# First token chunk of an attention + gated-MLP kernel: transposes in PSUM tiles of their own, the third block's statistics later, the first norm in one piece

## Chip, core and metric

The kernel runs on one core of one Trainium2 chip. The metric is the device time of one launch in microseconds (us), as the median of several runs. The kernel before was run six times: median 316.49, lowest 315.66, highest 317.83 us. The execution that was profiled is the one of 315.66 us; from its first to its last instruction, its span, it took 313.9 us, so 1.8 us of a run lie outside the span.

The engines are called by the profile's names: PE is TensorE (matmuls and transposes), PEld its weight loads, DVE is VectorE, ACT is ScalarE, POOL is GpSimd, and SP is the engine that issues most DMAs.

## What is computed

Input is `x` (2048 tokens of 640 features, bf16), normalised over the features, and then used in two branches, whose sum is added to `x`:

```python
xn = _layernorm(x)                              # (x - mean) / sqrt(var + 1e-5)
qkv = xn @ wqkv                                 # 32 heads of 20, q, k, v
scores = q @ k.T * 20 ** -0.5                   # each token sees itself and the 255 before it
o = softmax(masked scores) @ v
attention = o @ wo
g, u = xn @ w_gate, xn @ w_up                   # 640 -> 1536
mlp = (sigmoid(g) * u) @ w_down
out = x + attention + mlp
```

## The kernel before, in words

The 2048 tokens go through in four chunks of 512 (`CW`), each chunk in four blocks of 128 tokens (`SBC`). For the matmuls the normalised tokens must lie with features on the partitions: `xnT[c]`, 128 features x 5 groups x 512 tokens. For chunks 1 to 3 DMA transposes make it, beside other work. For chunk 0 nothing else is there to do yet, and the head of the program makes it on PE: this head is what the change is about.

The order of every engine's instructions is the order in which the Python code calls them (`tc.manual_schedule()`, L147), and each engine runs its own strictly in order. Tile pools only place buffers and add the waits: an instruction waits for the others that still use the tile that it writes or reads.

The head (L604 to L644) treats the four blocks of chunk 0 as follows.

- Mean and variance. Blocks 0 and 2 have theirs from DVE: two `bn_stats` of 320 features each (`ln_half`, L249) and one `bn_aggr` (`ln_mv`, L254); then ACT takes the square root (`root`, L579), and DVE the reciprocal (`norm`, L583). Blocks 1 and 3 have theirs from ACT: `mean_act` (L589, a copy that also sums), `root_act` (L594 and L595, squares and a root); DVE's reciprocal is at L599.
- The normalisation itself is one DVE `tensor_scalar` (L269 for blocks 0 and 2, L600 for 1 and 3) into `xn`. For block 0 it is cut in two pieces, features 0 to 383 and 384 to 639.
- `transpose_rows` (L275) has PE transpose the 128 x 128 squares of a block into PSUM, and `copy_rows` (L278) copies the result to `xnT`, with DVE or, for block 1, with ACT. For block 0 this goes in two rounds: three squares and their copy, then two squares and theirs.
- `project_v` (L324): for each block two groups of five matmuls that give the V columns 0 to 319 and 320 to 639 (`hf` 0 and 1), and `copy_v` (L331), which brings them to SBUF with DVE or ACT.

All transposes of the head write one PSUM tile, `home` (L608): 128 x 4 x 1024 bf16, 8 KB in each partition, so 2 KB for each block. It uses the buffer that the attention scores have later (pool `ps_s`, L145; tag "ps").

The inputs come by DMA (L173 to L201): block 0 of `x` on SP, blocks 1 and 2 on ACT, then on SP the V columns 0 to 319 of `wqkv`, block 3, the V columns 320 to 639, the q columns, the k columns, the first halves of `w_gate` and `w_up`, and two clears of scratch in DRAM.

After the head, PE makes q and k of chunk 0 without a pause: `g_qk(0)`, L298, 50 matmuls. Their results go through five SBUF buffers (`st`) to DRAM scratch (`sq`, `sk`, L306) and back in another layout (`qT`, `kT`, L313). Then gate and up matmuls (L398, L405) follow, and from L465 on the attention scores, mixed with matmuls of the other parts by a list with costs (`Fill`, L526). The change doesn't touch that part.

The lines of the head in their order, which is also DVE's, ACT's and PE's order:

```python
mv0 = ln_block(0, 0)                                  # L609
...
half2 = ln_half(0, 2, 0)                              # L612
r1 = root_act(1, xn1, neg1)
norm(0, mv0, r0, ((0, 3 * P), (3 * P, D)))            # L614
for lo, hi in ((0, 3), (3, DC)):
    transpose_rows(0, home, lo, hi)
    copy_rows(0, home, dve, lo, hi)
...
mv2 = ln_mv(ln_half(0, 2, 1, half2))                  # L623
```

Of the kernel before, what the change touches and what calls it, by code (L numbers as in the profile page):

```python
# [9 lines left out]
P = 128  # L10
S = 2048
D = 640
# [3 lines left out]
DC = D // P  # L16
FC = F // P
CW = 512
NCH = S // CW
SBC = CW // P  # L20
HG = 4
# [9 lines left out]
MULT = mybir.AluOpType.mult  # L31
SUB = mybir.AluOpType.subtract
POW = mybir.AluOpType.pow
GE = mybir.AluOpType.is_ge
BF16 = mybir.dt.bfloat16
FP32 = mybir.dt.float32
# [71 lines left out]
def kernel(  # L108
# [11 lines left out]
    nc = tc.nc  # L120
# [21 lines left out]
    ps_a = pool("ps_a", 1, space=bass.MemoryType.PSUM)  # L142
    ps_d = pool("ps_d", 3, space=bass.MemoryType.PSUM)
    banks = ctx.enter_context(ExitStack())
    ps_s = banks.enter_context(tc.tile_pool(name="ps_s", bufs=1, space=bass.MemoryType.PSUM))  # L145

    ctx.enter_context(tc.manual_schedule())  # L147

# [1 line left out]
    xc = {}  # L150

    def load_x(c):
        t = xp.tile([P, SBC, D], BF16, name="xc")
        xc[c] = t
        nc.sync.dma_start(out=t, in_=xr[:, c * SBC:(c + 1) * SBC, :])
# [73 lines left out]
    ident = const.tile([P, P], BF16, name="ident")  # L229
# [7 lines left out]
    for n in (6, 5):  # L237
        ps = ps_d.tile([P, CW], FP32, name="pwarm", tag="d")
# [4 lines left out]
    xnT = {}  # L243
    xns = {}

    def ln_half(c, s, a, stats=None):
        if a == 0:
            stats = lnp.tile([P, 2, nc.vector.BN_STATS_DIM], FP32, name="stats")
        nc.vector.bn_stats(out=stats[:, a, :], in_=xc[c][:, s, a * HALF:(a + 1) * HALF])  # L249
        return stats  # L250

    def ln_mv(stats):
        mv = lnp.tile([P, nc.vector.BN_AGGR_DIM], FP32, name="mv")
        nc.vector.bn_aggr(out=mv, in_=stats)  # L254
        return mv

    def ln_block(c, s):
        return ln_mv(ln_half(c, s, 1, ln_half(c, s, 0)))
# [4 lines left out]
        nc.gpsimd.tensor_tensor(out=rstd, in0=rstd, in1=neghalf, op=POW)  # L263
        return rstd

    def norm_block(c, s, mv, rstd, cuts=((0, D),)):
        xn = lnp.tile([P, D], BF16, name="xn", bufs=5)
        for a, b in cuts:
            nc.vector.tensor_scalar(out=xn[:, a:b], in0=xc[c][:, s, a:b], scalar1=mv[:, 0:1],  # L269
                                    scalar2=rstd[:, 0:1], op0=SUB, op1=MULT)  # L270
        xns[c, s] = xn

    def transpose_rows(s, home, lo=0, hi=DC):
        for d in range(lo, hi):
            nc.tensor.transpose(home[:, s, d * P:(d + 1) * P], xns[0, s][:, d * P:(d + 1) * P], ident)  # L275

    def copy_rows(s, home, copy, lo=0, hi=DC):
        copy(out=xnT[0][:, lo:hi, s * P:(s + 1) * P],  # L278
             in_=home[:, s, lo * P:hi * P].rearrange("p (d t) -> p d t", t=P))

    def turn_block(c, s):
        nc.sync.dma_start(out=xnT[c][:, :, s * P:(s + 1) * P], in_=xns.pop((c, s)), transpose=True)
# [8 lines left out]
    def proj_block(w, c, m):  # L291


        base = 0 if w == "q" else D
        ps = ps_d.tile([P, CW], FP32, name="pqk", tag="d")
        for d in range(DC):
            wt = wqkv[:, d, base:base + D].rearrange("p (k m) -> p m k", m=DC)
            nc.tensor.matmul(ps, lhsT=wt[:, m, :], rhs=xnT[c][:, d, :],  # L298
                             start=(d == 0), stop=(d == DC - 1))
        st = stp.tile([P, CW], BF16, name="st")  # L300
        if w == "q":
            nc.vector.tensor_copy(out=st, in_=ps)
        else:
            nc.scalar.copy(out=st, in_=ps)
        dst = scratch[w, c % 2].rearrange("(h j) s -> h j s", j=32)
        nc.sync.dma_start(out=dst[:, 4 * m:4 * m + 4, :], in_=st)  # L306

    def spread(w, c, g0, g1):

        if g0 == 0:  # L310
            qk[w, c] = (qp if w == "q" else kp).tile([P, NG, CW], BF16, name=w + "T")
        src = scratch[w, c % 2].rearrange("(g p) s -> p g s", p=P)
        nc.sync.dma_start(out=qk[w, c][:, g0:g1, :], in_=src[:, g0:g1, :])  # L313
# [7 lines left out]
    def project_v(c, s, hf):  # L321
        ps = ps_d.tile([P, CW], FP32, name="pv", tag="d")
        for d in range(DC):
            nc.tensor.matmul(ps[:, 0:HALF], lhsT=xnT[c][:, d, s * P:(s + 1) * P],  # L324
                             rhs=wqkv[:, d, 2 * D + hf * HALF:2 * D + (hf + 1) * HALF],
                             start=(d == 0), stop=(d == DC - 1))
        return ps
# [34 lines left out]
    def g_qk(c):  # L362
        for w in "qk":
            for m in range(DC):
                proj_block(w, c, m)
                if c == 0 and w == "q" and m == 1:
                    load_x(1)
                if w == "k" and m == 1:
                    spread("q", c, 0, NG if c else 2)
                yield 5 * MM  # L370
        if c == 0:
            spread("k", c, 0, 1)
            spread("k", c, 1, 3)
            spread("q", c, 2, 4)
            spread("k", c, 3, 4)
# [81 lines left out]

    def scores(c, step):
        pt = pp.tile([P, HG, PTW], BF16, name="pT")
        ps = ps_s.tile([P, HG, CW], FP32, name="ps", tag="ps")  # L460
        for g, hf, r, q, n, col in step["scores"]:
            kc, kb = divmod(c * SBC + r, SBC)
            key = kb * P + hf * U
            for i in range(HG):
                nc.tensor.matmul(  # L465
                    ps[hf * U:(hf + 1) * U, i, col * U:(col + n) * U],
                    lhsT=qk["k", kc][32 * i:32 * i + DH, g, key:key + U],
                    rhs=qk["q", c][32 * i:32 * i + DH, g, q * U:(q + n) * U],
                    start=True, stop=True)
        nc.scalar.activation(out=pt[:, :, 0:CW], in_=ps, func=EXP, scale=SCALE)  # L470

        def keep(out, in_, n, width, base, sign):
            nc.gpsimd.affine_select(out=out, in_=in_, pattern=[[0, HG], [0, n], [sign, width]],  # L473
                                    compare_op=GE, fill=0.0, base=base, channel_multiplier=-sign)

        def spans(u, n, units):
            a, b = divmod(u, SPAN)
            two = pt.rearrange("p h (a b) -> p h a b", a=2)
            return two[:, :, a:a + n, b * U:(b + units) * U]

        if "late" in step:
            src, to, n = step["late"]
            keep(pt[:, :, to * U:(to + n) * U].rearrange("p h (n u) -> p h n u", u=U),
                 spans(src, n, 1), n, U, -1 - U, -1)
            u, n = step["oldest"]
            keep(spans(u, n, 1), spans(u, n, 1), n, U, -1, -1)
            keep(spans(step["diag"], 2, 2), spans(step["diag"], 2, 2), 2, P, 0, 1)
        return pt
# [88 lines left out]
    def root(mv):  # L577
        r = lnp.tile([P, 1], FP32, name="rstd")
        nc.scalar.activation(out=r, in_=mv[:, 1:2], func=SQRT, bias=eps)  # L579
        return r  # L580

    def norm(s, mv, r, cuts=((0, D),)):
        nc.vector.reciprocal(r, r)  # L583
        norm_block(0, s, mv, r, cuts)

    def mean_act(s):
        xn = lnp.tile([P, D], BF16, name="xn", bufs=5)
        neg = lnp.tile([P, 1], FP32, name="neg")
        nc.scalar.activation(out=xn, in_=xc[0][:, s, :], func=IDENTITY, scale=-1.0 / D, accum_out=neg)  # L589
        return xn, neg  # L590

    def root_act(s, xn, neg):
        r = lnp.tile([P, 1], FP32, name="rstd")
        nc.scalar.activation(out=xn, in_=xc[0][:, s, :], func=SQUARE, bias=neg, accum_out=r)  # L594
        nc.scalar.activation(out=r, in_=r, func=SQRT, bias=eps, scale=1.0 / D)  # L595
        return r
# [8 lines left out]
    for s in range(SBC):  # L605
        new_v(0, s)
    act, dve = nc.scalar.copy, nc.vector.tensor_copy
    home = ps_s.tile([P, HG, 2 * CW], BF16, name="pt", tag="ps")  # L608
    mv0 = ln_block(0, 0)  # L609
    xn1, neg1 = mean_act(1)  # L610
    r0 = root(mv0)
    half2 = ln_half(0, 2, 0)  # L612
    r1 = root_act(1, xn1, neg1)
    norm(0, mv0, r0, ((0, 3 * P), (3 * P, D)))  # L614
    for lo, hi in ((0, 3), (3, DC)):
        transpose_rows(0, home, lo, hi)
        copy_rows(0, home, dve, lo, hi)
    v00 = project_v(0, 0, 0)
    norm_act(1, xn1, neg1, r1)
    xn3, neg3 = mean_act(3)  # L620
    transpose_rows(1, home)
    copy_rows(1, home, act)
    mv2 = ln_mv(ln_half(0, 2, 1, half2))  # L623
    r2 = root(mv2)
    v01 = project_v(0, 0, 1)
    copy_v(0, 0, 0, v00, dve)
# [1 line left out]
    r3 = root_act(3, xn3, neg3)  # L628
    v10 = project_v(0, 1, 0)
    copy_v(0, 0, 1, v01, dve)  # L630
    transpose_rows(2, home)
    copy_rows(2, home, dve)
    v11 = project_v(0, 1, 1)
    norm_act(3, xn3, neg3, r3)
    copy_v(0, 1, 0, v10, act)
    copy_v(0, 1, 1, v11, act)
    v20 = project_v(0, 2, 0)
    transpose_rows(3, home)
    copy_rows(3, home, dve)
    copy_v(0, 2, 0, v20, act)  # L640
    proj_v(0, 2, 1, dve)
    proj_v(0, 3, 0, act)
    proj_v(0, 3, 1, dve)
    nc.scalar.activation(out=scr, in_=neghalf, func=EXP)  # L644
    for _ in g_qk(0):
        pass
    load_rest()
# [37 lines left out]
    cuts = [(ends[n, NG - 1] + 2, f"out{n}") for n in range(NCH - 1)] + [(len(todo), None)]  # L685
# [23 lines left out]
    c = NCH - 1  # L709
# [17 lines left out]
    s = SBC - 1  # L727
    cuts = (HALVES[0], (HALF, 4 * P), (4 * P, D))
# [40 lines left out]
```

## Time and profile before

| | us |
|---|---|
| six runs: median (lowest to highest) | 316.49 (315.66 to 317.83) |
| the profiled execution: its time | 315.66 |
| its span | 313.9 |
| PE busy in the span | 308.0 |
| PE idle between its warm-up matmuls and its first transpose | 1.17 |
| PE busy in 7.2 to 14.5 us (7.3 us) | 7.07 |
| PE busy in 14.5 to 25.3 us, q and k of chunk 0 (10.8 us) | 10.80 |

Times in the profile count from the first instruction. The chain of waits follows the work that ended last back from the end, at each step to what released it; printed in order of time, a line has its start, its length and the instruction. The timeline lists instructions in order of time: start, length, engine, line, operation, out<-in, shapes; in square brackets how long the engine had been idle before it, and what ended that. [...] The granted TensorE clock was 1.000 over the whole span.

### The profile page before, as it was taken

The numbers are of one execution on the slowest core, as the hardware profiler recorded it, in microseconds if no ns is written. First come the engines' busy times: TensorE is split into PE (matmuls) and PEld (weight loads), VectorE is DVE, ScalarE is ACT, GpSimd is POOL, SyncE is SP. The second block draws the span as 40 slices with busy tenths as digits, with TensorE's granted clock in tenths as the row PEclk, the third lists the DMA queues.
The fourth block names the chain that finished last, engine by engine and source line by source line (L and its number), as shares of the span: only waits on it lengthen the run. The fifth ranks groups of instructions, "written<-read, shape, count | busy, mean of one in ns | idle before, by whom it ended". The sixth has DMA issues, their size and how long they took to land.

```text
span 313.9 us, 10569 instructions
## 1 busy us (share of the span) xinstructions
PE 308.0 (98%) x4664; PEld 175.8 (56%) x4664; DVE 158.5 (50%) x317; ACT 192.2 (61%) x177; POOL 159.6 (51%) x257
## 2 busy tenths in 40 slices
PE   6999999999999999999999999999999999999996
PEld 2554444456566656544566656544456664444674
DVE  4641486654865553447943552454452433673234
ACT  5614786788754468677654458776765657777100
POOL 3000387676778447355945536355355655565300
PEclk9999999999999999999999999999999999999999
DMA  7986999626913156500054035600000010000002
GB/s 246 375 277 189 321 378 176 221 84 188 237 47 78 46 175 195 164 2 0 2 53 80 23 108 155 200 2 3 2 2 23 23 44 2 4 0 4 1 2 84
DMA packets 35213, 33.08 MB, mean 105 GB/s; under 512 B 9920, under 2 KB 34624, under 8 KB 35136
## 3 DMA queue, kind: packets, MB, share of 16 engines
q1 hardware_dynamic: 34592, 31.97, 35.0%
q8 instruction: 36, 0.59, 0.8%
q10 hardware_dynamic: 576, 0.44, 0.4%
q14 instruction: 9, 0.07, 0.1%
HBM read 21.00 MB, written 10.26 MB: 100 GB/s over the span
## 4 chain that ended last, share of the span: by engine, by line
PE 96%; DMA 1%; DVE 1%; ACT 0%; issue 0%; ACTq 0%
PE pg L398 17%; PE pu L405 17%; PE y L419 15%; PE pqk L298 14%; PE ps L465 9%; PE acc L497 8%; PE pv L324 7%; PE y L426 6%; PE d L419 2%; DMA xc<-in_A_x_dram 1%; PE d L426 1%; PE pt L275 1%; PE acc L419 0%; ACT xnT L278 0%; DVE stats L249 0%
## 5 line engine op out<-in xcount | busy, mean ns | idle before, releaser
L473 POOL TENSOR_SCALAR_AFFINE_SELECT pT<-pT 128x512 bf16<-128x512 bf16 (+2 forms) x192 | 145.3, 787 | 132.6 <-ACT pT L470 132.5
L470 ACT ACTIVATE pT<-ps 128x2048 bf16<-128x2048 f32 x76 | 142.7, 1877 | 63.5 <-PE ps L465 59.1
L409 DVE SCALAR_TENSOR_TENSOR h<-th,pu 128x512 bf16<-128x512 f32 x48 | 32.8, 684 | 53.8 <-PE pu L405 32.2
L405 PE MATMUL pu<-xnT,wu 128*128 128x512 bf16 x240 | 59.8, 380 | 0.0
L398 PE MATMUL pg<-xnT,wg 128*128 128x512 bf16 x240 | 59.8, 380 | 0.0
L419 PE MATMUL y<-wd,h 128*128 128x320 bf16 (+1 forms) x348 | 50.2, 297 | 0.0
L298 PE MATMUL pqk<-xnT,wqkv 128*128 128x512 bf16 x200 | 46.0, 381 | 0.0
L419 PEld LDWEIGHTS <-h 128*128 128x128 bf16 x396 | 36.7, 98 | 14.3
L507 DVE STREAM_TRANSPOSE t<-acc 128x512 f32<-128x512 f32 x32 | 22.8, 713 | 34.3 <-PE acc L497 34.0
L401 ACT ACTIVATE th<-pg 128x512 f32<-128x512 f32 x48 | 28.6, 595 | 17.7 <-PE pg L398 12.0
L405 PEld LDWEIGHTS <-wu 128*128 128x128 bf16 x240 | 22.0, 98 | 25.6 <-issue 0.6
L398 PEld LDWEIGHTS <-wg 128*128 128x128 bf16 x240 | 22.0, 98 | 25.1 <-issue 0.4
L298 PEld LDWEIGHTS <-wqkv 128*128 128x128 bf16 x200 | 22.5, 119 | 18.1 <-issue 0.6
L465 PE MATMUL ps<-qT,kT 20*64 20x128 bf16 (+4 forms) x1856 | 32.5, 239 | 0.0
L465 PEld LDWEIGHTS <-kT 20*64 20x64 bf16 x1856 | 20.6, 104 | 19.1 <-issue 16.2
L430 DVE SCALAR_TENSOR_TENSOR xn<-y,xc 128x320 bf16<-128x320 f32 (+1 forms) x29 | 13.9, 483 | 29.4 <-PE y L426 29.4
L497 PEld LDWEIGHTS <-v 128*32 128x32 bf16 x1376 | 19.5, 97 | 13.6 <-issue 11.0
L497 PE MATMUL acc<-pT,v 128*32 128x64 bf16 (+3 forms) x1376 | 26.0, 223 | 0.0
L324 PE MATMUL pv<-wqkv,xnT 128*128 128x320 bf16 x160 | 24.2, 300 | 0.1
L519 DVE TENSOR_TENSOR on<-t,rec 128x320 bf16<-128x320 f32 (+4 forms) x48 | 22.2, 463 | 1.1
L426 PE MATMUL y<-wo,oc 128*128 128x320 bf16 (+1 forms) x145 | 21.6, 297 | 0.0
L426 PEld LDWEIGHTS <-oc 128*128 128x128 bf16 x165 | 15.6, 98 | 5.9
(49 smaller groups left out, 149.7 us busy)
## 6 DMA issues: line engine op xcount, KB each, us to landing
qT<-sq SPq DMA_DIRECT2D x3, 1024.0 KB, 5.7
sq<-st SPq DMA_DIRECT2D x20, 128.0 KB, 2.5
sk<-st SPq DMA_DIRECT2D x20, 128.0 KB, 4.8
out_dram<-xn SPq DMA_DIRECT2D x15, 160.0 KB, 1.8
kT<-sk SPq DMA_DIRECT2D x3, 768.0 KB, 5.0
wg<-in_B_w_gate_dram SPq DMA_DIRECT2D x2, 960.0 KB
wu<-in_B_w_up_dram SPq DMA_DIRECT2D x2, 960.0 KB, 9.3
xc<-in_A_x_dram SPq DMA_DIRECT2D x3, 640.0 KB, 5.5
```

The lines of the kernel that those rows point to most:

```text
L298: nc.tensor.matmul(ps, lhsT=wt[:, m, :], rhs=xnT[c][:, d, :], start=(d == 0), stop=(d == DC - 1))
L324: nc.tensor.matmul(ps[:, 0:HALF], lhsT=xnT[c][:, d, s * P:(s + 1) * P], rhs=wqkv[:, d, 2 * D + hf * HALF:2 * D + (hf + 1) * HALF], start=( ...
L398: nc.tensor.matmul(pg, lhsT=part(wg, d, f), rhs=xnT[c][:, d, :], start=(d == 0), stop=(d == DC - 1))
L401: nc.scalar.activation(out=th, in_=pg, func=TANH, scale=0.5)
L405: nc.tensor.matmul(pu, lhsT=part(wu, d, f), rhs=xnT[c][:, d, :], start=(d == 0), stop=(d == DC - 1))
L409: nc.vector.scalar_tensor_tensor(out=h, in0=th, scalar=1.0, in1=pu, op0=ADD, op1=MULT)
L419: nc.tensor.matmul(y[:, 0:cut[1] - cut[0]], lhsT=ht[c, f][:, s * P:(s + 1) * P], rhs=wd[:, f, cut[0]:cut[1]], start=(f == 0), stop=False)
L426: nc.tensor.matmul(y[:, 0:cut[1] - cut[0]], lhsT=oc[c, m][:, s * P:(s + 1) * P], rhs=wo[:, m, cut[0]:cut[1]], start=False, stop=(m == DC - 1))
L465: nc.tensor.matmul(ps[hf * U:(hf + 1) * U, i, col * U:(col + n) * U], lhsT=qk["k", kc][32 * i:32 * i + DH, g, key:key + U], rhs=qk["q", c] ...
L470: nc.scalar.activation(out=pt[:, :, 0:CW], in_=ps, func=EXP, scale=SCALE)
L473: nc.gpsimd.affine_select(out=out, in_=in_, pattern=[[0, HG], [0, n], [sign, width]], compare_op=GE, fill=0.0, base=base, channel_multipli ...
L497: nc.tensor.matmul(acc[32 * i:32 * i + 32, q * U:(q + n) * U], lhsT=v[:, h * VW:h * VW + 32], rhs=pt[:, i, col * U:(col + n) * U], start=( ...
```

## The change

Three things change in the head; the pools' text changes with them.

1. `home` goes. A new PSUM pool `ps_h` with four buffers stands where `ps_s` stood, and each call of `transpose_rows` takes a tile of 1280 bytes in each partition from it. So block 0, which calls it twice, has two tiles, and blocks 1, 2 and 3 one each. The fifth tile takes the buffer of the first. As built, the five stand in PSUM banks 4, 7, 6, 5 and 4. `ps_h` is closed at the end of the head, and `ps_s`, in the same four banks, is opened there.
2. Both `bn_stats` of block 2 stand with its `bn_aggr` in one place (L623), on DVE behind the normalisation of block 1. Before, the first of them stood ahead of the reciprocal of block 0.
3. The normalisation of block 0 is one instruction of 640 features in place of two of 384 and 256.

No other instruction is added, removed or moved on any engine, DMAs included. Compared instruction by instruction with their waits, the two built programs differ in three places: DVE's order around (2) and (3); PE's second round of transposes, which no longer waits for DVE's copy of the first; and ACT's copy of block 1, which no longer waits for DVE.

```diff
-    ps_s = banks.enter_context(tc.tile_pool(name="ps_s", bufs=1, space=bass.MemoryType.PSUM))
+    ps_h = banks.enter_context(tc.tile_pool(name="ps_h", bufs=4, space=bass.MemoryType.PSUM))
...
-    def norm_block(c, s, mv, rstd, cuts=((0, D),)):
+    def norm_block(c, s, mv, rstd):
         xn = lnp.tile([P, D], BF16, name="xn", bufs=5)
-        for a, b in cuts:
-            nc.vector.tensor_scalar(out=xn[:, a:b], in0=xc[c][:, s, a:b], scalar1=mv[:, 0:1],
-                                    scalar2=rstd[:, 0:1], op0=SUB, op1=MULT)
+        nc.vector.tensor_scalar(out=xn, in0=xc[c][:, s, :], scalar1=mv[:, 0:1],
+                                scalar2=rstd[:, 0:1], op0=SUB, op1=MULT)
         xns[c, s] = xn
 
-    def transpose_rows(s, home, lo=0, hi=DC):
+    def transpose_rows(s, copy, lo=0, hi=DC):
+        pt = ps_h.tile([P, DC, P], BF16, name="pt")
         for d in range(lo, hi):
-            nc.tensor.transpose(home[:, s, d * P:(d + 1) * P], xns[0, s][:, d * P:(d + 1) * P], ident)
-
-    def copy_rows(s, home, copy, lo=0, hi=DC):
-        copy(out=xnT[0][:, lo:hi, s * P:(s + 1) * P],
-             in_=home[:, s, lo * P:hi * P].rearrange("p (d t) -> p d t", t=P))
+            nc.tensor.transpose(pt[:, d, :], xns[0, s][:, d * P:(d + 1) * P], ident)
+        copy(out=xnT[0][:, lo:hi, s * P:(s + 1) * P], in_=pt[:, lo:hi, :])
...
-    home = ps_s.tile([P, HG, 2 * CW], BF16, name="pt", tag="ps")
     mv0 = ln_block(0, 0)
     xn1, neg1 = mean_act(1)
     r0 = root(mv0)
-    half2 = ln_half(0, 2, 0)
     r1 = root_act(1, xn1, neg1)
-    norm(0, mv0, r0, ((0, 3 * P), (3 * P, D)))
+    norm(0, mv0, r0)
     for lo, hi in ((0, 3), (3, DC)):
-        transpose_rows(0, home, lo, hi)
-        copy_rows(0, home, dve, lo, hi)
+        transpose_rows(0, dve, lo, hi)
     v00 = project_v(0, 0, 0)
     norm_act(1, xn1, neg1, r1)
     xn3, neg3 = mean_act(3)
-    transpose_rows(1, home)
-    copy_rows(1, home, act)
-    mv2 = ln_mv(ln_half(0, 2, 1, half2))
+    transpose_rows(1, act)
+    mv2 = ln_block(0, 2)
     r2 = root(mv2)
...
+    banks.close()
+    ps_s = banks.enter_context(tc.tile_pool(name="ps_s", bufs=1, space=bass.MemoryType.PSUM))
     for _ in g_qk(0):
         pass
```

## The prediction, made before the changed kernel ran

> **What bounds the kernel now.** I read the page first: busy times and the chain's shares.
>
> ```profile
> span 313.9 us, 10569 instructions
> PE 308.0 (98%) x4664; PEld 175.8 (56%) x4664; DVE 158.5 (50%) x317; ACT 192.2 (61%) x177; POOL 159.6 (51%) x257
> PE 96%; DMA 1%; DVE 1%; ACT 0%; issue 0%; ACTq 0%
> ```
>
> PE is the bound nearly everywhere, and the 4% of the chain that is not PE is some 12 us. So the place to look at is where the chain leaves PE. In order of time it does so only in the head:
>
> ```profile
> 1.24 3.98 DMA xc<-in_A_x_dram
> ...
> 5.25 0.49 DVE stats L249
> 5.74 0.07 DVE rstd L583
> ...
> 6.28 0.35 PE pt L275 x3
> ...
> 6.66 0.37 DVE xnT L278
> ...
> 7.07 0.29 PE pt L275 x2
> ...
> 8.77 0.70 ACT xnT L278
> ...
> 14.68 10.79 PE pqk L298 x50
> ```
>
> The load of block 2 of x ends at 5.22, DVE takes that block's first statistics (0.49), and only behind them, in DVE's order, comes block 0's reciprocal, which leads to all that follows. The two transposes at 7.07 hang on DVE's copy of the first three. From 14.68 on PE runs without a gap for long. What is gained or lost before that moves the rest of the program, unless a DMA that keeps its own time becomes due. The timeline has each link:
>
> ```profile
> 4.83 0.30 ACT L579 ACTIVATE rstd<-mv,eps 128x1 f32<-128x1 f32 x1 [0.15 <-DVE mv L254]
> 5.66 0.15 DVE L583 RECIPROCAL rstd<-rstd 128x1 f32<-128x1 f32 x1
> 7.07 0.27 PE L275 MATMUL pt<-ident,xn 128*128 128x128 bf16 x2 [0.45 <-DVE xnT L278]
> 7.38 0.29 DVE L278 COPY xnT<-pt 128x256 bf16<-128x256 bf16 x1 [0.36 <-PE pt L275]
> 7.78 0.45 DVE L600 TENSOR_SCALAR xn<-xc,neg,rstd 128x640 bf16<-128x640 bf16 x1
> 8.28 0.45 PE L275 MATMUL pt<-ident,xn 128*128 128x128 bf16 x5
> 8.77 0.69 ACT L278 COPY xnT<-pt 128x640 bf16<-128x640 bf16 x1 [1.79 <-PE pt L275]
> 9.69 0.16 DVE L583 RECIPROCAL rstd<-rstd 128x1 f32<-128x1 f32 x1 [0.46 <-ACT rstd L579]
> ```
>
> Block 0's root was ready at 4.83 + 0.30 = 5.13, and its reciprocal ran at 5.66.
>
> **Part 1, the statistics of block 2 out of the way.** Block 2's reciprocal started 0.03 after its root ended (9.36 + 0.30 to 9.69). By that row block 0's starts at 5.16, not at 5.66: 0.50 us earlier.
>
> **Part 2, the norm in one piece.** Before, the first transposes started 0.05 after the piece of 384 (0.38). A norm of 640 takes 0.446 (L269, block 2), so they start 0.07 later against the reciprocal: at 5.84 in place of 6.28, and the first copy likewise at 6.22 in place of 6.66. Up to here 0.50 - 0.07 = 0.43 to 0.44. In exchange DVE is done with the norm 0.19 sooner (0.64 for both pieces), which nobody waits for.
>
> **Part 3, tiles of their own.** PE's five transposes now run in one go (0.45 for five, as at 8.28), so the last is done at about 6.29, while DVE still does the first copy. The second copy then follows the first on DVE. Before it started 0.72 behind it (6.66 to 7.38). How closely it follows has no row of exactly this pair: consecutive statistics of 0.48 start 0.41 apart (3.67 to 4.08), so they overlap by 0.07, and with that a copy of 0.36 is followed after 0.28; without any overlap after 0.36. I take 0.28, the value of the nearest row, and keep 0.36 for the range. So the second copy moves from 7.38 to 6.50: 0.44 from here, 0.88 in all (0.80 at the other end). A gain beyond this is excluded, since PE and the copies have no other wait in this stretch.
>
> [...] Block 0's five squares had one 2 KB slot of `home`, and the row above has PE held 0.45 for DVE there. [...]
>
> **What the 0.88 passes through.** The reciprocal of block 1 (L599) follows the second copy after 0.21 as before, at 6.71; its root was ready at 5.97 + 0.29 = 6.26, so that is no new wait. Norm of block 1 at 6.90, transposes at 7.40 in place of 8.28, ACT's copy at 7.89 in place of 8.77 (ACT has had nothing to do since 6.99). Four things could be late next.
>
> - V columns 320 to 639 for PE's next matmuls. They are issued at 2.28 and take 5.5 to land, so 7.78; PE would come to them at 8.57 - 0.88 = 7.69. It waits some 0.13 (0.09 and 0.05 for the release), then needs five times 0.133 and is done at 8.49. Its next matmuls need ACT's copy and start at 9.52 - 0.88 = 8.64 anyway. This costs nothing, with 0.15 to spare.
> - Block 2's statistics, now two instead of one behind block 1's norm. Queued behind them on DVE are the V copy, block 2's reciprocal and its norm, for which PE waits at 10.39. They start at 8.14 - 0.88 = 7.26; two and the aggregate take 1.13 (3.67 to 4.80), so mean and variance are there at 8.39. ACT takes the root behind its copy, at 9.36 - 0.88 = 8.48. The V copy starts at 8.30 and ends at 8.74, the reciprocal is due at 8.81. Both fit, by 0.09 and 0.07; that cover gone, each 0.1 late costs 0.1.
> - q and k columns landed at 10.0 and 12.3 (issue at 2.75 and 3.32, 7.2 and 8.9 to land); they are used from 13.6 and 19. No cost.
> - The way of q and k through DRAM, below.
>
> So PE starts q and k at 14.52 - 0.88 = 13.64.
>
> **DMAs behind the head.** In the issues by line the first q writes and the V loads stand so, and one wait of ACT shows what they lead to:
>
> ```profile
> sq<-st SPq DMA_DIRECT2D x5, 128.0 KB, 3.7
> wqkv<-in_A_wqkv_dram SPq DMA_DIRECT2D x2, 400.0 KB, 5.5
> 24.09 1.07 ACT L304 CAST st<-pqk 128x512 bf16<-128x512 f32 x2 [1.24 <-DMA sq<-st]
> ```
>
> The third k cast waits until 23.99, when the third q write has landed and its `st` buffer is free. [...] POOL's and ACT's queues are not touched. The next in line are the first scores: kT had landed at 30.69, and they are due at 31.88 - 0.88 = 31.00, so even a kT that does not move at all is in time. The second half of `w_up` landed at 40.38 and is due at 40.9.
>
> **Sum.** 0.50 - 0.07 + 0.45 = 0.88, with 0.88 - 0.08 - 0.12 = 0.68 at the low end. The profiled execution of 315.66 (span 313.9) becomes 314.8 (span 313.0). It is the fastest of the six; against their median, 316.49 - 0.88 = 315.6. That is 0.28%. A measurement of this kernel can tell about 0.5% (1.6 us) from no change, so I forecast "within", on the fast side.
>
> **Rivals.**
>
> 1. Block 2 of x lands later in other executions. It held up the reciprocal, and in the fastest execution it landed at 5.22. The median lies 0.83 above that execution; if all of this is a later landing of block 2, the changed kernel, which needs it only at 7.26, gets it back as well: 316.49 - 0.88 - 0.83 = 314.8. For it: in DVE's order that load stands ahead of block 0's reciprocal, and in the profile it comes last of what the reciprocal needs. Against it: a late start of all loads is as good an explanation, and the change gains nothing on that.
> 2. Only part of it arrives, by the second statistics (0.07 to spare), by V columns a bit later than 7.78, or because a wait stays: gain 0.1 to 0.5, 316.0 to 316.4.
> 3. Slower: the way of q and k through DRAM, at SP's queue and the first scores (L465). The q writes, put in earlier, meet the weights and clears, and the order in which writes and the x load share the DMA engines comes out worse. The price: the q and k writes took from 2.3 to 4.3 to land, and the last k write, for which kT's load waits, took 2.3. With 4.3 kT lands at 32.7 in place of 30.7, 1.7 after the scores are due: 316.49 - 0.88 + 1.7 = 317.3. It decides from a kT that lands after 31.88, 1.2 later than now. Against it: those writes are issued when the DMA engines have room.
>
> **Chances and range.** Forecast as summed 0.60, rival 1 0.20, rival 2 0.12, rival 3 0.08. The medians of a few runs scatter by some 0.5 to 1 (six runs: 2.2 from end to end). The range from 314.4 to 316.9 holds the forecast's scatter, most of rival 1 and all of rival 2, and leaves rival 3 out. Faster than 314.9: most of rival 1 and a tail of the forecast, 0.24. Slower than 318.1: the worse part of rival 3 and what I have not thought of, 0.06. Within: 0.70.
>
> **What would show it.** Block 0's reciprocal at about 5.16, without statistics ahead of it; first transposes near 5.84, five in a row with no wait for DVE; second copy within 0.3 to 0.4 of the first; block 1's transposes near 7.40; ACT's root of block 2 directly behind its copy; PE's first q matmul near 13.6; first scores near 31.0, with no wait ahead of them. I am wrong if the first q matmul has moved and the scores have not (rival 3), if block 2's root or norm is what PE waits for (rival 2), or if the head gains what I say but the runs gain double (rival 1).

## The result, and the profile after

The changed kernel took 315.02 us in the median of 30 runs (314.59 to 316.12); the kernel before, measured beside it and counted with its earlier runs, 315.95 in the median of 68 (315.42 to 317.83). The ratio of the two is 0.9966, with a 95% interval from 0.9956 to 0.9975, so 1.07 us (0.8 to 1.4) were gained where 0.88 were forecast; the medians differ by 0.93. It is within the 0.5% named in advance, on the fast side. Two comparisons of the numbers say more than the median: the lowest runs differ by 0.83, close to the forecast, and 14 of the 68 runs before lie at 317.0 or above, while no run of the changed kernel does.

The first profile of the changed kernel is of its longest run, 316.12, with a span of 314.4. A second profile, taken later with the same kernel (after_again), is of a run of 314.82, with a span of 313.1. The second comes first here, in its timeline for DVE and PE. Line numbers are a few lower than before (L580 was L583, L268 L269, L276 L278, L321 L324).

```profile
5.11 0.16 DVE L580 RECIPROCAL rstd<-rstd 128x1 f32<-128x1 f32 x1 [0.36 <-ACT rstd L576]
5.31 0.45 DVE L268 TENSOR_SCALAR xn<-xc,mv,rstd 128x640 bf16<-128x640 bf16 x1
6.19 0.56 DVE L276 COPY xnT<-pt 128x384 bf16<-128x384 bf16 x2 [0.44 <-PE pt L275]
6.66 0.15 DVE L596 RECIPROCAL rstd<-rstd 128x1 f32<-128x1 f32 x1
6.85 0.45 DVE L597 TENSOR_SCALAR xn<-xc,neg,rstd 128x640 bf16<-128x640 bf16 x1
7.21 0.88 DVE L249 BATCH_NORM_STATS2 stats<-xc 128x6 f32<-128x320 bf16 x2
```

```profile
5.81 0.45 PE L275 MATMUL pt<-ident,xn 128*128 128x128 bf16 x5
6.61 0.85 PE L321 MATMUL pv<-wqkv,xnT 128*128 128x320 bf16 x5 [0.34 <-DVE xnT L276]
7.35 0.45 PE L275 MATMUL pt<-ident,xn 128*128 128x128 bf16 x5
8.18 0.99 PE L321 MATMUL pv<-wqkv,xnT 128*128 128x320 bf16 x6 [0.38 <-DMA wqkv<-in_A_wqkv_dram]
```

The reciprocal now waits for ACT's root alone (5.11, before 5.66). The five transposes run in one go, and the two copies need 0.56 together, so the second starts 0.27 behind the first (0.72 before). Block 1 is transposed at 7.35, before at 8.28.

The first profile has two things more. From its page:

```profile
span 314.4 us, 10567 instructions
PE 93%; DMA 4%; SPq 1%; DVE 0%; issue 0%; ACT 0%
```

The DMA share of the chain is 4% in place of 1%. This is its timeline for PE, at the head and where that DMA ends:

```profile
4.64 1.49 PE L240 MATMUL pwarm<-st 128*128 128x512 bf16 x3
5.92 0.71 PE L275 MATMUL pt<-ident,xn 128*128 128x128 bf16 x5
...
7.65 0.45 PE L275 MATMUL pt<-ident,xn 128*128 128x128 bf16 x5
```

```profile
42.32 1.04 PE L402 MATMUL pu<-xnT,wu 128*128 128x512 bf16 x4 [1.09 <-DMA wu<-in_B_w_up_dram]
```

PE came to its full clock only at 6.46 in that execution, 2.5 us later than in the profile before, so the first transposes took 0.71 for five in place of 0.45 and block 1 followed 0.30 later than in the second profile (0.06 of it because x landed later). And PE waited 1.09 us for the second half of `w_up`, which landed at 42.27 (before at 40.38). Neither is in the second profile of the same kernel.

### The profile page after: what moved, and what is told of

It is laid out like the page before. It is cut to its first block, busy times and chain, and to the rows that moved or that the text cites. A ratio compares the mean times of both kernels' runs of the same rounds, so it can differ in the third digit from the quotient of the medians.

```text
span 314.4 us, 10567 instructions
## 1 busy us (share of the span) xinstructions
PE 308.9 (98%) x4664; PEld 176.2 (56%) x4664; DVE 159.2 (51%) x316; ACT 192.3 (61%) x177; POOL 159.7 (51%) x257
## 4 chain that ended last, share of the span: by engine, by line
PE 93%; DMA 4%; SPq 1%; DVE 0%; issue 0%; ACT 0%
PE y L416 15%; PE pg L395 15%; PE pu L402 15%; PE pqk L295 14%; PE ps L462 8%; PE acc L494 7%; PE pv L321 7%; PE y L423 6%; DMA wu<-in_B_w_up_dram 4%; PE d L416 2%; PE pwarm L240 2%; DMA sk<-st 1%; PE d L423 1%; SPq L310 1%; PE pt L275 0%; PE acc L416 0%
## 5 line engine op out<-in xcount | busy, mean ns | idle before, releaser
L321 PE MATMUL pv<-wqkv,xnT 128*128 128x320 bf16 x160 | 24.1, 300 | 0.3 <-DVE xnT L276 0.3
L516 DVE TENSOR_TENSOR on<-t,rec 128x320 bf16<-128x320 f32 (+4 forms) x48 | 23.6, 492 | 1.1
```

## Experiments

Each kernel was measured beside the kernel before on the same chip; ratios are to it, with 95% intervals. Medians of the kernel before were 315.87 (67 runs, beside the first four), 316.10 (49, beside the second four) and 316.36 (59, beside the last). Each run has a mean granted TensorE clock. Its records begin with the rise to full clock, at 3.95 in the profile before, so the 1.000 given there leaves out what lies ahead: the warm-up matmuls took 0.61 to 0.64 us each until 3.79, and 0.38 from 4.08 on.

**One part alone, one part undone.** tiles_only, from the changed kernel:

```diff
+    half2 = ln_half(0, 2, 0)                       # early again
...
+    norm(0, mv0, r0, ((0, 3 * P), (3 * P, D)))     # in two pieces again
...
+    mv2 = ln_mv(ln_half(0, 2, 1, half2))
```

> Tiles of their own alone; the early statistics of block 2 and the norm in two pieces stay as before. My theory (three separate links of one chain, and their sum): the second copy follows the first at once, gain 0.44 us, ratio to the kernel before 0.9986. Rival (the wait of PE for the copy was not what held the second copy): gain under 0.1. A second question is the upper end of the kernel before, where 14 of 68 runs lie at 317.0 to 317.8 while none of 30 of the changed kernel does: if the later start of PE in the head makes it, it should be seen here, with block 0's reciprocal still at 5.66, in some of the runs.

Measured: 0.9981 (0.9964 to 0.9998), median 315.56. The interval, 0.1 to 1.1 us, holds the forecast of 0.44 and says no more; what happened is visible in the copies, here in DVE's timeline:

```profile
5.02 0.49 DVE L249 BATCH_NORM_STATS2 stats<-xc 128x6 f32<-128x320 bf16 x1
5.44 0.14 DVE L581 RECIPROCAL rstd<-rstd 128x1 f32<-128x1 f32 x1
5.61 0.64 DVE L269 TENSOR_SCALAR xn<-xc,mv,rstd 128x384 bf16<-128x384 bf16 x2
6.43 0.55 DVE L277 COPY xnT<-pt 128x384 bf16<-128x384 bf16 x2 [0.18 <-PE pt L276]
```

The reciprocal stands 0.42 behind the start of the statistics, as before, and both copies follow each other (0.55 for two). Two of 21 runs lie above 317, one of them with a lowered clock (0.994).

stats_only, from the kernel before:

```diff
-    half2 = ln_half(0, 2, 0)
...
-    mv2 = ln_mv(ln_half(0, 2, 1, half2))
+    mv2 = ln_block(0, 2)
```

> Both statistics of block 2 behind block 1's norm alone; one tile for all transposes and the norm in two pieces stay. My theory: block 0's reciprocal at 5.16 in place of 5.66, gain 0.50 us, ratio 0.9984, and the second transposes still wait for DVE. Rival (the load of block 2 makes the upper end of the runs of before): the gain of the median is the same, but no run lies at 317 or above. If it is the gap of PE that makes that end, it is thinned too, since PE starts 0.5 earlier.

Measured: 0.9980 (0.9968 to 0.9992), median 315.43, none of 21 runs above 316.82. The reciprocal ran at 5.13, with block 2 landing at 5.42, and PE's second transposes still waited for DVE (0.45). Both statements on the upper end hold, so this run can't tell the load from the gap of PE.

cuts_back, from the changed kernel:

```diff
-    norm(0, mv0, r0)
+    norm(0, mv0, r0, ((0, 3 * P), (3 * P, D)))
```

> The changed kernel with the norm of block 0 in two pieces again. My theory: the first transposes start 0.07 earlier (5.78 against 5.84 at the same clock) and everything behind them too, DVE's extra 0.19 is hidden: 0.07 faster than the changed kernel, ratio to before 0.9964, which the times alone can't tell from it. Rival (the extra DVE instruction delays the copies): slower than the changed kernel by 0.1 to 0.2.

Measured: 0.9971 (0.9957 to 0.9984), median 315.09: not to be told from the changed kernel, as forecast. In its profile the first transposes start 0.64 after the reciprocal and 0.70 in after_again, so 0.06 of the 0.07 is there.

home_kept, the changed kernel with `home` as before:

```diff
+    home = ps_s.tile([P, HG, 2 * CW], BF16, name="pt", tag="ps")
...
-        transpose_rows(0, dve, lo, hi)
+        transpose_rows(0, home, lo, hi)
+        copy_rows(0, home, dve, lo, hi)
...
```

> The changed kernel with one tile for all transposes again (statistics later, norm in one piece). My theory: PE's second transposes wait for DVE's first copy again, some 0.45, and 0.44 of the gain is lost: ratio to before 0.9986. Rival (the wait is hidden behind something else): as the changed kernel, 0.9966.

Measured: 0.9989 (0.9974 to 1.0005), median 315.55. The times alone hardly tell it from either kernel; the wait came back, in PE's timeline:

```profile
5.95 0.34 PE L275 MATMUL pt<-ident,xn 128*128 128x128 bf16 x3 [0.29 <-DVE xn L269]
6.74 0.27 PE L275 MATMUL pt<-ident,xn 128*128 128x128 bf16 x2 [0.45 <-DVE xnT L278]
```

**What makes the upper end of the runs before.** Of the 175 runs of the kernel before whose clock is known, 41 have a mean granted clock of 0.993 to 0.995; their medians in the three groups are 317.4 to 317.6, those of the others 315.8 to 315.9. They are 35 of the 43 runs at 317.0 or above. The other eight, up to 319.14, show 1.000; so would a run without clock records, as two of the fourteen profiles here are (home_kept and cuts_back), and what made these eight long stays open. None of the 53 such runs of the changed kernel is below 0.999. Four experiments ask what takes the clock away.

before_long_warm, from the kernel before, and after_short_warm, from the changed one:

```diff
-    for n in (6, 5):
+    for n in (6, 8):        # before_long_warm;  after_short_warm: (6, 2)
```

> The kernel before with 14 in place of 11 warm-up matmuls, so that PE is busy until about 5.8 at the full clock and the gap ahead of its first transpose shrinks from 1.17 to 0.5. Theory clock: the runs of before at 317.0 to 317.8 are those in which PE stays at half its clock for one more stretch of the head, because the gap counted as idle; with the gap filled they disappear, and the median stays (315.9 to 316.0). Where PE is at half clock through all 14, they end near 7.2 and delay the transposes by up to 0.9, which would lift the median by 0.1 to 0.5. Rival, landing of block 2 of x: the upper end stays at about one run in five, since no load is changed.

Measured: 0.9994 (0.9974 to 1.0013), median 316.53 against 316.10, 315.49 to 317.42. None of 14 runs had a clock below 0.999, while 14 of 49 of the kernel before had beside them. So with a longer warm-up the drop is gone, but the median lies 0.6 above those runs of before that kept the clock (315.92). That a warm-up that ends later costs this was expected, and isn't shown. The only profile is of the run of 317.42, at full clock from its rise on, and it shows another delay: PE was through with the warm-up at 6.83 and idle for 0.84 after it; block 2 of x landed at 6.63, and DVE's timeline shows what hung on it:

```profile
6.65 0.49 DVE L249 BATCH_NORM_STATS2 stats<-xc 128x6 f32<-128x320 bf16 x1 [2.02 <-DMA xc<-in_A_x_dram]
7.06 0.15 DVE L583 RECIPROCAL rstd<-rstd 128x1 f32<-128x1 f32 x1
```

That is 1.40 later than in the profile before, with the load issued at the same time.

> The changed kernel with 8 in place of 11 warm-up matmuls, so that the gap of PE ahead of its first transpose is 1.2 or more again, as in the kernel before. Theory clock: an upper end of the runs 1.5 to 2 above the rest appears, in one run in five or more, and its mean granted clock is lower by 0.004 to 0.006. Rival, landing of block 2: as the changed kernel, nothing above 316.2.

Measured: 0.9982 (0.9968 to 0.9997), median 315.87, 314.68 to 316.59. The forecast failed: no run had a low clock, yet the median lies 0.7 above that of after_late_x2 beside it (315.20). short_warm_look was to show the cause:

> One look more at the changed kernel with 8 warm-up matmuls, whose median was 315.87 without the drop of the mean clock that theory clock had forecast; its first profile was of a run at the fast end, 314.7, with full clock from 4.1 on. In two runs out of three this one should be of the slower kind (315.7 or more). Theory: there the full clock comes one stretch later (7.5 or so), and the transposes and V matmuls before it show twice their time. Rival: the clock comes as early, and the time lies elsewhere.

It fell on a run of 314.74, at the lower end, with full clock from 4.2 on, so it shows nothing of the longer runs. Why fewer warm-up matmuls cost this stays open. In the first profile the clock held (1.00 from 7.49 to 10.90) with PE idle for 1.23 ahead of its first transposes, more than in the profile before, and busy for 1.84 of the 3.41 us behind the rise.

before_late_x2 and after_late_x2, the same edit in either kernel:

```diff
-    load_rows(2, nc.scalar)
     load_v(0)
     load_rows(3, nc.sync)
+    load_rows(2, nc.sync)
     load_v(1)
```

> The kernel before with the load of block 2 of x issued on SP behind the first V columns and block 3, in place of third on ACT. It should land near 6.5 in place of 5.2. My theory of part 1 (block 2's statistics hold up block 0's reciprocal): the reciprocal goes to about 7.0 and all behind it by some 1.2 to 1.3, median 317.2. Rival (DVE's order costs only the 0.49 of the instruction itself): no change.

Measured: 1.0045 (1.0022 to 1.0067), median 317.99, so 1.9 longer where 1.2 to 1.3 were expected. Block 2 landed at 6.32 and the reciprocal ran at 6.75, behind its statistics as before. The rest goes with the clock: 9 of 11 runs have 0.993 to 0.995, and the two that have not, 317.10 and 317.33, lie 1.2 and 1.4 above the runs of before that kept the clock (315.92). The busy time of PE by stretches of 3.41 us from its profile, with the granted clock behind it (then DMA share and GB/s):

```profile
2.35:5.76 3.41, 3.41 (x9) 1.00 1.04 335
5.76:9.17 3.41, 1.60 (x11) 1.00 1.08 378
9.17:12.59 3.42, 3.31 (x17) 0.50 1.07 369
```

The clock rose at 5.76 (the row ahead of it has 1.00 for want of a record); in the 3.41 us that followed PE was busy for 1.60, with 1.36 idle ahead of its first transposes alone; and for the next 3.41 us it had half the clock (0.50; 1.00 again from 12.60 on). Half a clock over 3.41 us of nearly unbroken work would be 1.7 us, an estimate from these rows. In the kernel before, the runs with a low clock are 1.5 to 1.7 longer in the medians; here the nine lie only 0.8 above the two, in the median, and why it is less stays open. The same stretches in the profile before, where the clock held:

```profile
3.95:7.36 3.41, 1.80 (x13) 1.00 1.07 347
7.36:10.78 3.42, 3.19 (x26) 1.00 1.04 371
```

And in after_again:

```profile
5.44:8.85 3.41, 2.69 (x22) 1.00 1.06 356
8.85:12.27 3.42, 3.42 (x32) 1.00 1.06 377
```

Behind 1.80 busy of 3.41 the clock held, behind 1.60 it fell, and the changed kernel had 2.69. These rows leave a rival, the longest single gap (1.36 where the clock was lost, 1.17 where it held). The ends of two other profiles speak against it. PE's last work ends inside each of them. First the changed kernel's first profile, then tiles_only:

```profile
310.25:313.66 3.41, 1.30 (x22) 1.00 0.32 96
313.66:314.40 0.74, 0.00 (x0) 0.50 0.00 0
```

```profile
308.38:311.79 3.41, 2.00 (x27) 1.00 0.44 142
311.79:313.20 1.41, 0.00 (x0) 1.00 0.01 1
```

In tiles_only PE was idle for the last 1.41 of its stretch, longer than the 1.36, but busy for 2.00, and the clock held. In the other eleven profiles with clock records PE was busy for 1.80 to 3.29 of the 3.41 us behind the rise, and the next stretch had full clock in each. No stretch between 1.60 and 1.80 was seen, so where between them the clock goes down isn't shown. One such stretch at half clock is 0.0054 of a span of 314 us, which makes a mean of 0.995, an estimate from these rows; by it the runs with a low mean (0.993 to 0.995) had about one, but where it lay only this one profile shows.

> The same later load of block 2 in the changed kernel, where its statistics are due at about 7.2. My theory: it has landed by then, and the median stays that of the changed kernel, 315.0, within 0.2. Rival (the later load shifts the V columns or block 3 as well and it is those that count): slower by 0.3 or more.

Measured: 0.9956 (0.9937 to 0.9976), median 315.20, none of 15 runs with a low clock. With block 2 landing at 6.32 the changed kernel is what it was. In this pair the same late load cost 1.9 us and came with a low clock in 9 of 11 runs where the reciprocal stands behind it in DVE's order, and nothing that the times can tell where it doesn't (315.20, no low clock in 15 runs).

**What spreads the runs of the changed kernel.** after_again:

> The changed kernel itself once more, as a second sample: its first profile has a span of 314.4, near the top of its runs, with PE waiting 1.1 us for the second half of w_up. Theory: that wait and the half clock at the first transposes are of that execution; this profile should have a span of 312.9 to 313.5, the first q matmul near 13.6, and no or a shorter wait for w_up. Ratio to before 0.9966 within 0.001, and no run with a mean granted clock of 0.995 or lower. Rival (the wait belongs to the change, since PE comes to w_up 0.9 earlier): 0.5 or more of it here too.

Measured: 0.9963 (0.9948 to 0.9978), median 315.42, 314.52 to 316.98, no low clock in 22 runs. Span 313.1 and first q matmul at 13.67, as forecast, and no wait for `w_up` but one of 0.38 for the V columns, shown above. Its trace lacks 35 matmul records, all behind 14 us, so its PE sums are not used there.

after_split_wu, with a helper that loads columns a to b of the second half:

```diff
-        for k in range(1, F // FS):
-            load_gu(k)
+        load_gu_part(1, 0, FS // 2)
         spread("q", 0, 4, NG)
         spread("k", 0, 4, NG)
+        load_gu_part(1, FS // 2, FS)
```

> The changed kernel with the second half of w_gate and w_up loaded in two parts, the columns needed first ahead of the q and k loads, the others behind them. Theory: the wait for w_up is what spreads the runs of the changed kernel from 314.6 to 316.1, so with its first columns landing some 2 to 4 us earlier the spread shrinks to under 0.8 and the median falls by 0.2 to 0.4, to 314.7. Rival (the wait is rare, and the spread is made in the first 8 us by the loads and the clock): median and spread as the changed kernel.

Measured: 0.9955 (0.9940 to 0.9971), median 315.27, 314.70 to 316.45. The first columns landed at 36.5, some 3 us sooner than the whole half in after_again (39.8), as planned; the spread stayed as wide. The forecast failed: the wait for `w_up` is not what spreads the runs.

> Both together: norm of block 0 in two pieces and the split load of the second half of w_gate and w_up. If both help it is the fastest: 314.6, ratio to before 0.995; if neither does, the changed kernel's 0.9966 within 0.001.

Measured: 0.9969 (0.9954 to 0.9985), median 315.32. Neither of them beats the changed kernel by anything that the times can tell.

## Why the prediction was right

**Statistics out of the way, 0.50.** Right. The reciprocal moved from 5.66 to 5.11 in after_again; with all loads 0.05 earlier there (root at 4.78, not 4.83), that is 0.50. stats_only shows it without the other edits.

**Norm in one piece, 0.07 lost.** Right: 0.70 from reciprocal to first transposes (5.11 to 5.81), 0.62 before (5.66 to 6.28), so 0.08.

**Tiles of their own, 0.45.** Right, and the nearest row was the right one to take: the second copy starts 0.27 behind the first, 0.28 was assumed. That the wait would go altogether was my estimate. That it belongs to the shared tile is shown from both sides, by tiles_only without it and by home_kept, where it is back with its 0.45. The bank isn't told apart from the tile: as built, block 0's two tiles also lie in two banks (4 and 7), and no run has two tiles in one bank. So whether a tile of its own in the same bank would have freed PE was not shown.

**What could be late next.** The V columns landed at 8.14 in after_again, not at 7.78, and PE waited 0.38 for them. (V matmuls in a row start 0.136 apart in the profile before; I had put 0.133.) Of that only 0.09 got through: the transposes of block 2 started at 9.55 where their norm had let them go at 9.46. ACT's root of block 2 ran at 8.43 (8.48 forecast), behind its copy. First q matmul at 13.67, where 13.64 was forecast. So the head is 0.85 shorter than in the profile before.

**DMAs behind it.** The load of chunk 1, issued from 18.16 before and landed at 23.68, was issued from 17.32 and landed at 22.78, 0.90 earlier, and kT at 29.90, 0.79 earlier: both moved with their issue. Not all did: the second q write was issued 0.84 earlier than before (16.75, 17.59 before) and landed 0.36 later (21.05, 20.69 before). That reached ACT, whose first k cast was due at 21.19 - 0.88 = 20.31 and waited for the first q write:

```profile
20.82 1.19 ACT L301 CAST st<-pqk 128x512 bf16<-128x512 f32 x2 [5.69 <-DMA sq<-st]
```

PE didn't wait for it, and the third k cast, at 24.09 before, ran at 23.21, 0.88 earlier. No run shows the 0.12 that the low end of the sum takes off, a wait of PE for that cast; in its place after_again has the cast earlier by the whole 0.88 and no such wait. The slower rival did not come about, and the first scores had no wait for kT in either profile of the changed kernel. What could cost something was the second half of `w_up`, which I had put at 40.4 against a need at 40.9: in one profile of two it landed at 42.27. I had taken its landing from one execution as if it were fixed. after_split_wu says that it isn't the rule.

**The first rival had a true core and a wrong price.** Block 2 of x does land at different times: 5.00 to 6.63 in twelve profiles with the load in its old place. In the kernel before that goes straight into the reciprocal; in the changed kernel it doesn't, as the pair with the late load shows. The measured 315.02 even lies nearer to this rival's 314.8 than to the forecast's 315.6. But that is the starting point: the kernel before had 316.49 in six runs and 315.95 in 68, and 315.95 - 0.88 = 315.07.

I had priced the rival at its delay alone. What both sums lacked is the clock: the later the reciprocal, the longer PE's gap (1.17 with the reciprocal at 5.66, 1.36 with it at 6.75), and in before_late_x2, where PE was busy for 1.60 of a stretch of 3.41 us, the next stretch ran at half clock. Of the 59 runs of before beside after_again 18 had a low mean clock. They lie 1.49 above the others in the mean (317.59 and 316.10), which is 18/59 x 1.49 = 0.45 for all 59. The means of the two kernels differ by 1.18 there (316.55 and 315.37); without the low runs 0.73 is left, for which the forecast of 0.88 is a little high. The interval is some 0.5 us to each side, so the two shares are an account that fits and no measurement of each. That the medians differ by just 0.93 is in part luck, for a median shows little of what a quarter of the runs lose.

**Open.** Which of the two edits keeps the clock up: in stats_only, cuts_back and home_kept no run of 56 was low, in tiles_only one of 21, and either edit shortens the gaps of PE. Also what spreads the runs of the changed kernel over 1.5 to 2.5 us; a late rise of the clock alone doesn't, for the profiles of after_late_x2 and cuts_split_wu have it at 7.20 and 6.70 in runs of 315.06 and 315.13. And why a short warm-up costs 0.7.

## What to carry to other kernels

Where one engine works in strict order, look at what stands ahead of the step that all wait for: an early start of later work can tie the whole head to a load that is not needed yet (before, block 0's root was ready at 5.13 and its reciprocal ran at 5.66, behind statistics whose load landed at 5.22). Two halves that share a PSUM tile were tied to each other here even where they touched different columns (PE waited 0.45 for the copy, in the kernel before and in home_kept); with a tile, and a bank, of its own each went its way (no such wait in after_again). And a gap of PE in a short opening stage can cost more than its length: here one of 1.36 us, with one of 0.45 behind it, left PE busy for 1.60 of 3.41 us, and the next 3.41 us had half the clock.

## What the runs showed of the hardware

- In before_late_x2 the clock of PE was 0.50 from 9.17 to 12.59 us, after PE had been busy for 1.60 of the 3.41 us ahead of that; in the profile before, after 1.80, it did not fall. At the program's end it fell after 1.30 (first profile of the changed kernel) and held after 2.00 (tiles_only), there with a gap of 1.41. No stretch between 1.60 and 1.80 was seen, and only one profile shows the drop in the head.
- The rise to full clock came at 3.95 to 7.20 us in nine profiles with the same eleven warm-up matmuls from 1.25 on. Where it came at 6.46, the first five transposes took 0.71 in place of 0.45.
- One and the same load, block 2 of x, issued at 1.24 or 1.25 us, landed from 5.00 to 6.63 us in twelve profiles.
